# First product of nine of twelve token pairs as seven products of half sums, the verdict on VectorE and TensorE, and zeros in tiles of three PSUM groups

## The chip, the cores and the metric

The kernel runs on one core of a Trainium2 chip. A core has TensorE (PE in the profile; its weight loads are listed apart as PEld), VectorE (DVE), ScalarE (ACT), GpSimd (POOL) and SyncE (SP), which issues most of the DMAs. The metric is the device time of one execution in microseconds, lower is better. The kernel before took 631.13 us, the median of three runs (629.88, 631.13 and 631.83).

## The reference

Attention over a window, then a feed forward product over its output. Everything is fp32; batch 4, 8 heads, 768 positions, head dimension 64, so that `x` has 3072 tokens of 512 values. `n_global` is 8 and `n_local` is 96.

```python
scores = scale * np.matmul(q, k.transpose(0, 1, 3, 2))        # 4 x 8 x 768 x 768
keep = is_global | is_local                                   # first 8 keys, or the last 96
scores = np.where(keep, scores + bias, -1e9)                  # bias = -slope(head) * distance
a = np.exp(scores - max); a = a / (a.sum(-1) + 1e-9)
x = (a @ v) as 3072 x 512
h = x @ w_in                                                  # 512 -> 2048
g = np.where(h >= 1, h, np.where(h <= -1, 0, (h + 1) ** 2 / 4))
out = (g @ w_out).astype(np.float32)                          # 2048 -> 512
```

`w_in` and `w_out` arrive as float64.

## The kernel before, in words

**Tiles.** A unit is 128 query rows of one batch with all 8 heads, and there are 24. The first unit of each batch (units 0 to 3) sees 128 keys and is computed in fp32 (`first_scores`, `first_turn`, `first_av`, `first_xt`). The other 20 see 256 keys and are computed with each fp32 number as two fp16 numbers, a high and a low part, so that one product becomes three matmuls (high by high, high by low, low by high). A unit is worked in two halves of four heads: `scores` (L757, 24 matmuls of 128 columns on 64 rows), `masked` (L578, VectorE), `expo` (L590, ScalarE, which also adds up the row sums with an accumulator), `split_p` (L773 high part on ScalarE, L775 low part on VectorE), `turn_p` (a DMA transpose, L782), `attend` (L800, 24 matmuls of 64 columns), `norm` (L602), `scale_x` (L642), `split_x` (L814, L816) and `turn_x` (DMA transpose).

Two units make a pair of 256 tokens, and there are twelve. For each pair `ffn1` (L885) computes `h` in 8 groups, each with 24 matmuls of 256 columns (2 slices of 128 outputs, 4 of 128 inputs, 3 products of parts) into one PSUM tile of the group `ps_h`. `gelu` takes a tile through ScalarE (L898), VectorE (L903, L908), ScalarE (L912, the high part) and GpSimd (L916, the low part). `ffn2` (L928) multiplies by `w_out`: per pair 2 token blocks of 16 slices of 3 matmuls of 512 columns into `ps_o`. `finish` (L945, L943, L948) scales and stores.

**Weights.** The float64 weights come in 32 pieces (`w_load` L466), are put together from their two halves with integer operations on VectorE (`w_bits` L480, L484, L487), and split (`w_hi` L500 and `w_scale` L507 on ScalarE, `w_lo` L514 on GpSimd). While that goes on, the first pairs of FFN1 and FFN2 follow the pieces. From then on the pieces are loaded a second time for tests of their range (`check_load` L541, `check_reduce` L546).

**Order.** Every step is put into a list with a due time (`at`), and the list is run in the order of a written table of indices, `PLACE` (lines 103 to 249). The order of each engine's instructions is the order in that table. Nothing is reordered at run time; an instruction waits for its inputs and for its tile, and what stands behind it on its engine waits too. `filler` (L443) issues a matmul of zeros of 128x512 into the tile `spare`, which nobody reads, between the first steps.

**Verdict.** The kernel holds for inputs within bounds. At the end (L282 to L308) VectorE compares all recorded maxima with their limits, GpSimd reduces over partitions (L304), and one register is loaded (L308); if it is set, a general path is run, which is not the case here.

The lines the change touches:

Of the kernel before, what the change touches and what calls it, by code (L numbers as in the profile page):

```python
# [39 lines left out]
SC = SQK * SQK  # L40

# [4 lines left out]
NSU = NU // 2 * (NFC // 2)  # L46

NQ = "scalar"
WENG = "a"
INS = 6  # L50
F32B = 7
PSH = 2
PSO = 2
HB = {"k": 3, "q": 2, "v": 3}
HE = {"k": "p", "q": "p", "v": "v"}
KGE = "vector"
XL = "v"
# [263 lines left out]
def fast_path(ctx, tc, q, k, v, nraw, nval, w_in, w_out, out, half, nm, sums, sq, su):  # L321
# [900 lines left out]
```

## Time and profile before

| what | value |
|---|---|
| median of three runs | 631.13 us |
| span of the profiled execution, first to last instruction | 629.1 us |
| PE busy | 615.7 us, 98% |
| DVE busy | 448.0 us, 71% |
| ACT busy | 418.7 us, 67% |
| POOL busy | 239.5 us, 38% |
| granted TensorE clock, mean over the span | 0.999 |

The page gives for the profiled execution no time other than its span; the median of the runs is 2.0 us longer. A row of the page's fifth part names the source line, the engine, the operation and its tiles, then the busy time and the mean duration of one instruction, then the engine's idle time just before these and what ended it. Matmuls overlap, so the mean duration of a matmul (380 ns for 512 columns) is longer than the distance from one start to the next; the timeline shows the distance. In the timeline the first number is the start, the second the duration, and a bracket at the end names the idle time before the row.

### The profile page before, as it was taken

What the parts mean: (1) busy time and instruction counts of PE and PEld (TensorE: products, weight loads), DVE (VectorE), ACT (ScalarE), POOL (GpSimd) and SP (SyncE); (2) the same over time, 40 slices, a digit from 0 to 9 for tenths busy, and PEclk for the clock granted to TensorE, in tenths of its full rate; (3) what the DMA queues carried; (4) which work ended last, traced back from release to release, by engine and by line L of the source; (5) the groups of instructions that cost most, each with busy time, mean ns of one, the idle gap of its engine ahead of it and who ended that gap; (6) DMA issues with size and microseconds to landing.
All of it is one profiled execution on the core that took longest, in us unless ns stands there. A gap on an engine that the chain in (4) does not pass through costs nothing. (4 is left out here: it accounts for less than half of the span.)

```text
span 629.1 us, 14881 instructions
## 1 busy us (share of the span) xinstructions
PE 615.7 (98%) x5665; PEld 420.8 (67%) x5665; DVE 448.0 (71%) x1150; ACT 418.7 (67%) x1070; POOL 239.5 (38%) x226
## 2 busy tenths in 40 slices
PE   7999999899999999999999999999999999999996
PEld 4676666556876767767757667667667767767652
DVE  6889999987676656665777777777777686663440
ACT  4778898997777776676686776766866765632220
POOL 0336786650544424433443333425324421122210
PEclk9999999999999999999999999999999999999999
DMA  6847566597533553464395497586476455361121
GB/s 201 261 144 225 187 227 221 129 170 157 126 87 77 91 121 93 80 148 111 69 231 154 94 208 186 127 186 175 110 177 183 112 140 137 76 150 69 51 69 38
DMA packets 144227, 88.08 MB, mean 140 GB/s; under 512 B 108180, under 2 KB 124820, under 8 KB 144148
## 3 DMA queue, kind: packets, MB, share of 16 engines
q1 hardware_dynamic: 144000, 86.92, 55.4%
q8 instruction: 46, 0.75, 0.5%
q14 instruction: 33, 0.27, 0.1%
q10 hardware_dynamic: 148, 0.13, 0.1%
HBM read 54.53 MB, written 6.29 MB: 97 GB/s over the span
## 5 line engine op out<-in xcount | busy, mean ns | idle before, releaser
L885 PE MATMUL h<-xt,wih 128*128 128x256 f16 x1536 | 256.4, 273 | 1.0 <-DVE u L908 0.9
L916 POOL TENSOR_TENSOR gl<-u,gh 128x512 f16<-128x512 f32 x96 | 117.4, 1224 | 284.9 <-ACT gh L912 274.6
L885 PE MATMUL h<-xt,wil 128*128 128x256 f16 x768 | 209.4, 273 | 0.0
L885 PEld LDWEIGHTS <-wih 128*128 128x128 f16 x1536 | 147.4, 98 | 30.9 <-DVE u L908 1.6
L928 PE MATMUL o<-wol,gh 128*128 128x512 f16 x384 | 145.6, 379 | 1.3 <-POOL wol L514 1.2
L928 PE MATMUL o<-woh,gh 128*128 128x512 f16 x384 | 145.8, 380 | 0.0
L928 PE MATMUL o<-woh,gl 128*128 128x512 f16 x384 | 145.6, 379 | 0.0
L928 PEld LDWEIGHTS <-gh 128*128 128x128 f16 x768 | 71.8, 98 | 67.3
L903 DVE SCALAR_TENSOR_TENSOR h<-h,u 128x512 f32<-128x512 f32 x96 | 66.7, 694 | 68.2 <-ACT u L898 68.0
L590 ACT ACTIVATE z<-z,nm 128x256 f32<-128x256 f32 (+1 forms) x192 | 91.7, 479 | 14.9 <-DVE nm L578 14.3
L912 ACT ACTIVATE gh<-u 128x512 f16<-128x512 f32 x96 | 60.2, 627 | 60.4 <-DVE u L908 60.1
L898 ACT ACTIVATE u<-h,half 128x512 f32<-128x512 f32 x96 | 64.9, 676 | 43.3 <-PE h L885 43.2
L578 DVE CUSTOM_DVE_ANT_0 z<-s,bias 128x256 f32<-128x256 f32 (+1 forms) x192 | 67.2, 396 | 26.6 <-PE s L757 23.2
L885 PEld LDWEIGHTS <-wil 128*128 128x128 f16 x768 | 75.0, 98 | 8.8
L775 DVE SCALAR_TENSOR_TENSOR ph<-z,ph 128x1024 f16<-128x1024 f32 x40 | 60.0, 1499 | 22.1 <-ACT ph L773 21.8
L928 PEld LDWEIGHTS <-gl 128*128 128x128 f16 x384 | 37.5, 98 | 47.2 <-issue 2.2
L908 DVE SCALAR_TENSOR_TENSOR u<-u,h 128x512 f32<-128x512 f32 x96 | 65.3, 681 | 3.3 <-DVE good L298 0.3
L546 DVE TENSOR_REDUCE sq<-c_raw 128x1 f32<-128x256 f32 x128 | 48.6, 408 | 0.2
L773 ACT ACTIVATE ph<-z 128x1024 f16<-128x1024 f32 x40 | 42.0, 1050 | 0.7
L757 PEld LDWEIGHTS <-qh 64*128 64x128 f16 x960 | 26.9, 94 | 16.7 <-issue 9.5
L800 PEld LDWEIGHTS <-pt 128*128 128x128 f16 x960 | 33.4, 98 | 7.0
L590 ACT ACTIVATION_READ_ACCUMULATOR z<-z,nm 128x1 f32 x192 | 36.0, 187 | 0.0
(101 smaller groups left out, 676.6 us busy)
## 6 DMA issues: line engine op xcount, KB each, us to landing
w_raw<-in_moe_w_in_dram SPq DMA_DIRECT2D x16, 512.0 KB, 3.8
w_raw<-in_moe_w_out_dram SPq DMA_DIRECT2D x16, 512.0 KB, 3.7
c_raw<-in_moe_w_in_dram SPq DMA_DIRECT2D x32, 256.0 KB, 3.5
c_raw<-in_moe_w_out_dram SPq DMA_DIRECT2D x32, 256.0 KB, 3.1
vr<-in_v_dram SPq DMA_DIRECT2D x28, 256.0 KB, 3.5
kr<-in_k_dram SPq DMA_DIRECT2D x28, 256.0 KB, 3.7
qr<-in_q_dram SPq DMA_DIRECT2D x24, 256.0 KB, 4.0
out_dram<-ob SPq DMA_DIRECT2D x23, 256.0 KB, 3.0
```

The costliest lines, as they stand in the source:

```text
L546: nc.vector.tensor_reduce(sq[:, col : col + 1], tops[n, e], axis=AX.X, op=op, apply_absolute_value=True)
L578: nc.vector.tensor_tensor_reduce(out=p32[u, hf][:, hh, :], in0=pts[u, hf][hh // 2][:, hh % 2, 0:n], in1=bias[:, 4 * hf + hh, base : base + n],
L590: nc.scalar.activation(z, z, AF.Exp, bias=nm[:, c : c + 1], scale=-1.0, accum_out=sums[:, c : c + 1])
L773: nc.scalar.activation(phs[u, hf][:, 0, :], zf, AF.Copy, scale=SP_)
L775: nc.vector.scalar_tensor_tensor(phs[u, hf][:, 1, :], zf, SP_, phs[u, hf][:, 0, :], op0=ALU.mult, op1=ALU.subtract)
L885: nc.tensor.matmul(hp[:, e, :], w[:, dc, f], xt[:, hf, 2 * a + j, :], start=(n == 0), stop=(n == 3 * NDC - 1),)
L898: nc.scalar.activation(us[c, g], hs[c, g], AF.Relu, bias=half, scale=2.0 / (SV * SW), accum_out=su[:, col : col + 1])
L903: nc.vector.scalar_tensor_tensor(ws[c, g], hs[c, g], 4.0 / (SV * SW), us[c, g], op0=ALU.mult, op1=ALU.max)
L908: nc.vector.scalar_tensor_tensor(dst, us[c, g], 4.0, ws[c, g], op0=ALU.min, op1=ALU.mult)
L912: nc.scalar.activation(gh, ws[c, g], AF.Copy)
L916: (nc.gpsimd if GL == "p" else nc.vector).tensor_sub(gl, ws[c, g], gt[c, g][0])
L928: nc.tensor.matmul(po, a[:, cs], w[:, f, :], start=(f == 0 and n == 0), stop=(f == NFC - 1 and n == 2))
```

## The change

For pairs 3 to 11 `ffn1` is replaced by `product`, `keep` and `join`. The tokens of the pair are cut into two blocks of 128, the 512 inputs into two halves of 256, and the 256 outputs of a pair of slices into two of 128; seven products of sums of these blocks take the place of eight. Each half pair (`j`, 1024 of the 2048 outputs) has seven products of 24 matmuls of 128 columns, listed as p1, p5, p2, p6, p3, p7, p4; the table sets which of them come next to each other and what stands between. Four of the seven (p6, p7 and p4 in the tile of p1, p3 in that of p5) are accumulated on an earlier product in the same PSUM tile; p7's sum with p5 is written by VectorE into a fourth tile, and p4, which is accumulated in the tile that p7 used, follows that. `keep` copies a product to SBUF on ScalarE, `join` adds it on VectorE. Pairs 0 to 2 keep `ffn1`.

The sums have to be made: of the weights once (`t_sum` and `t_mix` on GpSimd, 8 and 32 instructions, `t_hi` on ScalarE, `t_lo` on VectorE, 8 x 2 each), of `x` for each of the nine pairs (`mix_x`, four instructions on GpSimd of 128x256). The parts of `x` are split into `xa` (128x512, the unchanged blocks) and `xb` (128x1280, the sums), with the low parts on GpSimd and no longer on VectorE, and each is turned by a DMA transpose.

Beside that: the row sums of units 4 to 23 come from a 65th column of ones in `attend`, not from an accumulator; the accumulator of `gelu`'s first step is gone; `turn_p` is two transposes, one behind each part; the PSUM group `ps_b` is gone and `ps_h` has 3 tiles; pairs 0 and 1 take FFN2 together while the weights arrive; fillers write tiles of three PSUM groups in turn and wait for these like any other step; and the verdict stands in the table, on VectorE, with a matmul on TensorE for the sum over partitions. The general path is not changed.

```diff
+FIRSTW = 3
+PRODUCTS = ("p1", "p5", "p2", "p6", "p3", "p7", "p4")
+XLO = "gpsimd"
+TMIX = "gpsimd"
+TLO = "vector"
...
-    ps_b = pool("ps_b", 1, space=PSUM)
-    ps_h = pool("ps_h", PSH, space=PSUM)
+    ps_h = pool("ps_h", 3, space=PSUM)
...
+    def filler(tag, n):
+        shape = [P, 2, WIN] if tag == "s" else [P, DM]
+        spare = {"s": ps_s, "h": ps_h, "o": ps_o}[tag].tile(shape, F32, tag=tag, name=f"spare_{tag}{n}")
...
+    def t_mix(g, n):
+        t = tsum[g]
...
+        b11, b12, b21, b22 = t[:, 0:2, 0], t[:, 0:2, 1], t[:, 2:4, 0], t[:, 2:4, 1]
+        dst, x, y = ((b11, b12, b11), (b12, b22, b12), (b22, b22, b11), (b21, b21, b22))[n]
+        getattr(nc, TMIX).tensor_sub(dst, x, y)
...
-        av = ps_av.tile([P, 4, D], F32, tag="av", name=f"av{u}_{hf}")
+        av = ps_av.tile([P, 4, D + 1], F32, tag="av", name=f"av{u}_{hf}")
...
+    def mix_x(c, n):
...
+        a11, a12, a21, a22, s1 = (xs[c][:, e, :] for e in range(5))
+        if n == 0:
+            nc.gpsimd.tensor_add(s1, a21, a22)
+        elif n == 1:
+            nc.gpsimd.tensor_sub(a21, a11, a21)
...
+    def product(c, j, name):
...
+        for m in range(4):
+            g = 4 * j + m
+            n = 0
+            for dc in range(2):
+                for a, b in ((0, 0), (0, 1), (1, 0)):
...
+                    nc.tensor.matmul(
+                        hp[:, m, :], w, xf(b, dc), start=(fresh and m == n == 0),
...
+    def keep(c, j, name):
...
+        s = mid.tile([P, 4 * P], F32, tag="m", name=f"s{name}_{c}_{j}")
+        nc.scalar.activation(s, flat(hs[c, j, {"p1": "a", "p6": "a", "p5": "b"}[name]]), AF.Copy)
...
+    def join(c, j, t):
+        slot, name, prod = {11: ("c", "p1", "p2"), 12: ("b", "p6", "p3"), 22: ("a", "p5", "p7")}[t]
...
+        if t == 22:
+            dst = flat(ps_h.tile([P, 4, P], F32, tag="h", name=f"h{c}_{j}d"))
...
+        nc.vector.tensor_add(dst, h, sc[c, j, name])
...
-    nc.gpsimd.partition_all_reduce(anybad, worst, channels=P, reduce_op=bass_isa.ReduceOp.max)
...
+    def sentence():
+        total = ps_av.tile([1, 1], F32, tag="av", name="total")
+        nc.tensor.matmul(total, worst[:, 0:1], worst[:, 1:2], start=True, stop=True)
+        nc.vector.tensor_single_scalar(badi, total, 0.5, op=ALU.is_ge)
```

The table `PLACE` is new throughout. Three places of the order that it sets, in the instructions as each engine gets them (line, operation, result<-operands, size of the result, and the queues of which a wait is written on the instruction):

On TensorE before, at the end of the second product of pair 6 (`o6_1`) and the beginning of the first product of pair 7 (`h7_6`):

```order
L928 LDWEIGHTS gh6_6_5536
L928 MATMUL o6_1_5621<-wol_119,gh6_6_5536 128x512
L928 LDWEIGHTS gl6_6_5569
L928 MATMUL o6_1_5621<-woh_118,gl6_6_5569 128x512
L885 LDWEIGHTS wih_116 [waits DVE_49]
L885 MATMUL h7_6_6199<-xt7_5071,wih_116 128x256 [waits PE_49]
```

TensorE after, at the place where p4 of pair 7's first half begins; six matmuls of FFN2 stand between it and the last matmul of p7, and the rows show the last two of them (`tt0_1` are half sums of weights, `xtb7` the turned sums of `x`, `h7_0a` the tile that p7 was accumulated in):

```order
L1039 LDWEIGHTS gh6_1_22_6604
L1039 MATMUL o6_1_6482<-wol_117,gh6_1_22_6604 128x512
L1039 LDWEIGHTS gl6_1_22_6605
L1039 MATMUL o6_1_6482<-woh_116,gl6_1_22_6605 128x512
L972 LDWEIGHTS tt0_1_1056
L972 MATMUL h7_0a_6571<-xtb7_6598,tt0_1_1056 128x128 [waits DVE_49]
```

Both times products of FFN1 follow matmuls of FFN2 of pair 6. Before, a new tile begins there, which waits for an earlier `gelu`; after, p4 goes on in the tile of p7 and waits for the join on VectorE that reads it.

On VectorE before, a stretch of the steady part (pair 7, units 16 to 18; `ph` is the low part of the probabilities):

```order
L775 SCALAR_TENSOR_TENSOR ph17_0_5953<-z17_0_5912,ph17_0_5953 128x1024 [waits DMAHW1_49,Activation_49]
L903 SCALAR_TENSOR_TENSOR h7_3_5917<-h7_3_5917,u7_3_5966 128x512 [waits Activation_49]
L642 TENSOR_TENSOR x16_1_6004<-av16_1_5971,r16_1_5740 128x256 [waits PE_49]
L908 SCALAR_TENSOR_TENSOR u7_3_5966<-u7_3_5966,h7_3_5917 128x512 [waits DVE_49,Pool_49]
L742 COPY vh16_3_5248<-vg2_4547 32x1024
L816 TENSOR_TENSOR xh16_1_6010<-x16_1_6004,xh16_1_6010 128x256 [waits DMAHW2_49,Activation_49]
L707 SCALAR_TENSOR_TENSOR vh18_5_6000<-vr18_5_5786,vh18_5_6000 128x512 [waits DMAHW5_49]
```

VectorE after, a like stretch (pair 7, units 18 and 19):

```order
L701 SCALAR_TENSOR_TENSOR vh19_0_7357<-vr19_0_7196,vh19_0_7357 128x8x64 [waits DMAHW7_49,Activation_49]
L997 TENSOR_TENSOR h7_1d_7407<-h7_1a_7027,sp5_7_1_7128 128x512 [waits PE_49]
L731 COPY vg3_7417<-vh19_0_7357 32x1040 [waits DVE_49,Pool_49]
L493 TENSOR_REDUCE sq_69<-c19_0_raw_7267 128x1
L1012 SCALAR_TENSOR_TENSOR h7_1d_7407<-h7_1d_7407,u7_1_22_7420 128x512 [waits Activation_49]
L493 TENSOR_REDUCE sq_69<-c19_1_raw_7294 128x1 [waits DMAHW5_49]
L775 SCALAR_TENSOR_TENSOR ph18_0_1_7481<-z18_0_7322,ph18_0_0_7447 128x1024 [waits DMAHW0_49,Activation_49]
L1014 SCALAR_TENSOR_TENSOR u7_1_22_7420<-u7_1_22_7420,h7_1d_7407 128x512 [waits DVE_49,Pool_49]
```

Joins (L997) stand between the steps of `gelu` and of attention, and the low half of `x` (L816) is gone from this engine.

On VectorE before, the end of the program (`good` and `worst` are the verdict, `ob` the last store):

```order
L298 TENSOR_SCALAR good_9090<-peak_9091 128x16 [waits DVE_49]
L301 TENSOR_REDUCE worst_9103<-good_9090 128x1 [waits DVE_49]
L302 TENSOR_SCALAR worst_9103<-worst_9103 128x1 [waits DVE_49]
L306 CAST badi_9108<-anybad_9106 128x1 [waits Pool_49]
L943 TENSOR_SCALAR ob11_1_9069<-o11_1_9015 128x256 [waits Activation_49]
```

VectorE after, its end (the join and the last steps of `gelu` of pair 11, then the threshold of the sum and the last store):

```order
L1110 MEMSET worst_70 128x1
L1111 TENSOR_REDUCE worst_70<-good_10549 128x1 [waits DVE_49]
L1112 TENSOR_SCALAR worst_70<-worst_70 128x1 [waits DVE_49]
L997 TENSOR_TENSOR h11_1d_10626<-h11_1a_10373,sp5_11_1_10459 128x512 [waits PE_49]
L1012 SCALAR_TENSOR_TENSOR h11_1d_10626<-h11_1d_10626,u11_1_22_10631 128x512 [waits Activation_49]
L1014 SCALAR_TENSOR_TENSOR u11_1_22_10631<-u11_1_22_10631,h11_1d_10626 128x512 [waits DVE_49,Pool_49]
L1012 SCALAR_TENSOR_TENSOR h11_1a_10373<-h11_1a_10373,u11_1_21_10662 128x512 [waits Activation_49]
L1014 SCALAR_TENSOR_TENSOR u11_1_21_10662<-u11_1_21_10662,h11_1a_10373 128x512 [waits DMAHW3_49,DVE_49]
L1117 TENSOR_SCALAR badi_71<-total_10740 1x1 [waits PE_49]
L1054 TENSOR_SCALAR ob11_1_10743<-o11_1_10622 128x256 [waits Activation_49]
```

The verdict's comparisons moved from behind all of pair 11 to a place ahead of its last join, and what waits for another engine at the very end is the threshold (L1117), for a matmul.

## Rows read from the trace of the kernel before

**Rows 1.** The page's first part for two engines, busy time, share of the span and instructions, and the granted clock of TensorE in 40 slices, in tenths.

```profile
PE 615.7 (98%) x5665; PEld 420.8 (67%) x5665; DVE 448.0 (71%) x1150; ACT 418.7 (67%) x1070; POOL 239.5 (38%) x226
...
PEclk9999999999999999999999999999999999999999
```

**Rows 2.** Busy time of the engines by stretch: length, then for each engine busy time and instructions, the granted clock, the DMA share and GB/s.

```profile
core 0: us, PE busy (x) PEld busy (x) DVE busy (x) ACT busy (x) POOL busy (x), PEclk, DMA share, GB/s
0.00:40.00 40.00, 35.91 (x210) 23.86 (x211) 30.92 (x133) 24.62 (x78) 8.38 (x12) 1.00 0.67 211
40.00:80.00 40.00, 38.67 (x284) 27.52 (x283) 39.47 (x85) 33.15 (x79) 26.95 (x26) 1.00 0.62 198
80.00:127.00 47.00, 44.74 (x417) 30.58 (x416) 45.63 (x96) 44.38 (x107) 32.85 (x29) 1.00 0.62 187
127.00:178.00 51.00, 50.90 (x565) 35.67 (x562) 38.62 (x102) 41.57 (x112) 21.05 (x21) 1.00 0.74 149
...
0.00:178.00 178.00, 170.23 (x1467) 117.63 (x1468) 154.65 (x413) 143.72 (x373) 89.23 (x87) 1.00 0.66 184
178.00:624.00 446.00, 445.49 (x4200) 303.17 (x4198) 292.97 (x737) 275.02 (x698) 150.23 (x139) 1.00 0.52 123
```

**Rows 3.** TensorE's timeline where the third pair's FFN1 ends (177.60) and in a stretch of the steady part.

```profile
177.60 0.27 PE L885 MATMUL h<-xt,wil 128*128 128x256 f16 x1
177.71 0.38 PE L928 MATMUL o<-woh,gh 128*128 128x512 f16 x1
...
202.31 0.86 PE L800 MATMUL av<-vh,pt 128*128 128x64 f16 x24
203.01 0.38 PE L928 MATMUL o<-woh,gh 128*128 128x512 f16 x1
...
204.31 0.38 PE L885 MATMUL h<-xt,wih 128*128 128x256 f16 x2
...
206.93 0.38 PE L928 MATMUL o<-woh,gh 128*128 128x512 f16 x1
...
209.30 0.38 PE L928 MATMUL o<-woh,gl 128*128 128x512 f16 x1
209.62 0.84 PE L757 MATMUL s<-kh,qh 64*128 64x128 f16 x24
210.39 0.39 PE L885 MATMUL h<-xt,wih 128*128 128x256 f16 x2
```

**Rows 4.** TensorE's groups by line and shape: instructions, busy time, mean ns of one, idle time before.

```profile
L885 PE MATMUL h<-xt,wih 128*128 128x256 f16 x1536 | 256.4, 273 | 1.0 <-DVE u L908 0.9
L885 PE MATMUL h<-xt,wil 128*128 128x256 f16 x768 | 209.4, 273 | 0.0
L928 PE MATMUL o<-woh,gh 128*128 128x512 f16 x384 | 145.8, 380 | 0.0
L800 PE MATMUL av<-vh,pt 128*128 128x64 f16 x960 | 34.5, 193 | 0.0
L800 PEld LDWEIGHTS <-pt 128*128 128x128 f16 x960 | 33.4, 98 | 7.0
L757 PE MATMUL s<-kh,qh 64*128 64x128 f16 x960 | 33.8, 217 | 0.0
L443 PE MATMUL spare<-zeros 128*128 128x512 f16 x109 | 30.5, 413 | 0.0
```

**Rows 5.** Groups of the other engines by line and shape, in the same columns.

```profile
L903 DVE SCALAR_TENSOR_TENSOR h<-h,u 128x512 f32<-128x512 f32 x96 | 66.7, 694 | 68.2 <-ACT u L898 68.0
L816 DVE TENSOR_TENSOR xh<-x,xh 128x256 f16<-128x256 f32 x40 | 19.4, 486 | 0.6 <-ACT xh L814 0.6
L775 DVE SCALAR_TENSOR_TENSOR ph<-z,ph 128x1024 f16<-128x1024 f32 x40 | 60.0, 1499 | 22.1 <-ACT ph L773 21.8
L912 ACT ACTIVATE gh<-u 128x512 f16<-128x512 f32 x96 | 60.2, 627 | 60.4 <-DVE u L908 60.1
L590 ACT ACTIVATION_READ_ACCUMULATOR z<-z,nm 128x1 f32 x192 | 36.0, 187 | 0.0
L898 ACT ACTIVATION_READ_ACCUMULATOR u<-h,half 128x1 f32 x96 | 18.4, 192 | 0.0
L916 POOL TENSOR_TENSOR gl<-u,gh 128x512 f16<-128x512 f32 x96 | 117.4, 1224 | 284.9 <-ACT gh L912 274.6 <-issue 6.4 <-PE o L928 3.9
```

**Rows 6.** The timeline of all engines from the last matmul of an FFN1 group to the first two steps of its `gelu`.

```profile
410.87 0.27 PE L885 MATMUL h<-xt,wil 128*128 128x256 f16 x1
...
411.18 0.69 ACT L898 ACTIVATE u<-h,half 128x512 f32<-128x512 f32 x1 [0.36 <-PE h L885]
411.76 0.19 ACT L898 ACTIVATION_READ_ACCUMULATOR u<-h,half 128x1 f32 x1
411.99 0.70 DVE L903 SCALAR_TENSOR_TENSOR h<-h,u 128x512 f32<-128x512 f32 x1 [0.52 <-ACT u L898]
```

**Rows 7.** The same timeline a little earlier, where VectorE's low part of the probabilities lies beside work of GpSimd, and that line's shortest, median and longest duration in ns.

```profile
406.39 1.16 POOL L713 TENSOR_TENSOR qh<-qr,qh 128x512 f16<-128x512 f32 x1
406.58 2.05 DVE L775 SCALAR_TENSOR_TENSOR ph<-z,ph 128x1024 f16<-128x1024 f32 x1 [1.08 <-ACT ph L773]
...
L775 DVE SCALAR_TENSOR_TENSOR ph<-z,ph x40: 1215/1226/2124, 108.3 to 550.2; 128x1024 f16<-128x1024 f32 x40
```

**Rows 8.** The timeline of the end, without FFN2, and a group of the program's start (a matmul of one row that VectorE reads).

```profile
613.38 0.38 POOL L304 PARTITION_ALL_REDUCE anybad<-worst  x1 [5.97 <-issue]
613.79 0.15 DVE L306 CAST badi<-anybad 128x1 int32<-128x1 f32 x1 [4.54 <-POOL anybad L304]
...
623.59 0.38 ACT L945 ACTIVATE ob<-o 128x256 f32<-128x256 f32 x1 [9.76 <-PEq L308]
...
L394 PE MATMUL pps_n<-nlow,bias 1*128 1x2 f32 x2 | 0.6, 359 | 1.2 <-DVE nlow L392 1.2
```

More of the change, by code (lines that the diff above doesn't have):

```diff
@@ L399, in distances @@
     def distances(own):
+        after("positions")
+        did.add(("dist", own))
         n = P if own else WIN
@@ L402, in distances @@
         m = zp.tile([P, 3, n], F32, tag="z", name=f"m{n}")
-        dist, gap, cut = (m[:, j] for j in range(3))
+        dist, gap = m[:, 0], m[:, 1]
         here = prow[:, 0:1] if own else prow[:, 1:2]
@@ L413, in clip @@
     def clip(own):
+        after("limits", ("dist", own))
+        did.add(("clip", own))
         n = P if own else WIN
@@ L473, in w_bits @@
         if s == 0:
-            if num < NFC and num % 2 and not TPO:
-                wbits[n] = spare(1).bitcast(I32).rearrange("p (a b) -> p a b", a=NDC)
-            else:
-                wbits[n] = ps_b.tile([P, *hi.shape[1:]], I32, tag="b", name=f"w{num}_bits")
+            p, tag = (ps_o, "o") if num < NFC and num % 2 >= BODD else (ps_h, "h")
+            wbits[n] = p.tile([P, *hi.shape[1:]], I32, tag=tag, name=f"w{num}_bits")
         t = wbits[n]
@@ new lines, in split_b, with turn_b @@
+    def split_b(c, lo):
+        after(*(("mix", c, n) for n in range(4)))
+        did.add(("xb", c, lo))
+        src = xs[c].rearrange("p a b -> p (a b)")
+        xbs[c, lo] = xp.tile([P, 5 * 4 * D], F16, tag=f"xb{lo}", name=f"xb{c}_{lo}")
+        if not lo:
+            nc.scalar.activation(xbs[c, 0], src, AF.Copy)
+        else:
+            low(XLO, xbs[c, 1], src, xbs[c, 0])
+    def turn_b(c, lo):
+        after(("xb", c, lo))
+        did.add(("xtb", c, lo))
+        if c not in xtbs:
+            xtbs[c] = xp.tile([P, 2, 5, 2, P], F16, tag="xt", bufs=2, name=f"xtb{c}")
+        nc.sync.dma_start_transpose(
+            out=xtbs[c][:, lo].rearrange("p b j d -> p (b j) d"), in_=xbs[c, lo]
+        )
@@ L919, in ffn2 @@
[L919 to L931 removed]
+        nm_ = f"{c}_{g}" if isinstance(g, int) else f"{c}_{g[0]}_{g[1]}"
@@ new lines, in ffn2 @@
+    def ffn2(c, t, f, n):
+        if c < FIRSTW:
+            g, e = divmod(f, 2)
+            key, cs = g, slice(e * CH + t * P, e * CH + (t + 1) * P)
+        else:
+            j, m = divmod(f, NFC // 2)
+            m, e = divmod(m, 2)
+            key, cs = (j, 10 * (t + 1) + e + 1), slice(m * P, (m + 1) * P)
+        after(("w", NFC + f), ("g", c, key, 4))
+        if n == 0:
+            p, tag = (ps_h, "h") if c == 1 else (ps_o, "o")
+            os_[c, t] = p.tile([P, DM], F32, tag=tag, name=f"o{c}_{t}")
+        gh, gl = gt[c, key]
+        for i, (a, w) in enumerate(((gh, woh), (gh, wol), (gl, woh))):
+            nc.tensor.matmul(
+                os_[c, t], a[:, cs], w[:, f, :], start=(n == 0 and i == 0), stop=(n == NFC - 1 and i == 2)
+            )
+        if n == NFC - 1:
@@ new lines, in fast_path @@
+    for J in range(J0, 2 * NCH):
+        first = J == J0 and FIRSTW == 2
+        tj[J + 1] = tj[J] + (11.5 if first else PJ)
+    for c in range(FIRSTW + 1, NCH + 1):
+        starts[c] = tj[2 * c]
+    for J in range(J0, 2 * NCH):
+        c, j = divmod(J, 2)
+        t, dt = tj[J], (tj[J + 1] - tj[J]) / 7
+        for n, name in enumerate(PRODUCTS):
+            tp = t + dt * n
+            at(tp, product, c, j, name)
+            if name in ("p1", "p5", "p6"):
+                at(tp + 1.5, keep, c, j, name)
+            d = {"p2": 11, "p3": 12, "p7": 22, "p4": 21}.get(name)
+            if d:
+                if d != 21:
+                    at(tp + 1.6, join, c, j, d)
+                put_gelu(c, (j, d), tp + 2.2)
+        last = J + 1 == 2 * NCH
+        t, dt = tj[J + 1] + 1.5, 0.66 if last else PJ / 16
+        order = [(x, e, m) for x in range(2) for e in ((0, 1) if x == 0 else (1, 0)) for m in range(4)]
+        for n, (x, e, m) in enumerate(order):
+            at(t + dt * n, ffn2, c, x, 8 * j + 2 * m + e, 8 * j + n % 8)
+            if j == 1 and n % 8 == 7:
+                put_finish(c, t + dt * n + 0.8, x)
```

766 lines of the change are left out of this document (420 added, 346 removed), and 308 rows, old and new, of tables (PLACE, k).

## The prediction

> **What bounds the kernel now.** I read the engines' shares first. TensorE is busy 98% of the span with the clock granted in full; VectorE has 71%, ScalarE 67%, GpSimd 38% [rows 1]. An average can hide stages, so the stretches come next [rows 2]. From 178 us to 624 TensorE is busy 445.49 of 446.00 us. Before that it is busy 170.23 of 178.00, fillers included, and VectorE has 85.10 of 87.00 us between 40 and 127, where the weights are converted. So there are two stages: the first, up to the end of the third pair's FFN1 at 177.7 [rows 3], shared by TensorE and VectorE; and the second, TensorE alone.
>
> Since matmuls overlap, their cost is the distance of starts, not the mean duration in the groups [rows 4]. The timeline gives it [rows 3]: 24 matmuls of 256 columns from 204.31 to 206.93, 109.2 ns each; 11 distances of 512 columns in 2.37 us, 215.5 ns each; 24 of `attend` (64 columns, a weight load each) in 0.70 us, 29.2 ns; 24 of `scores` in 0.77 us, 32.1 ns, or 64.2 for the two that share the row groups. With these, the second stage before is 960 x 0.2155 + 1728 x 0.1092 + 744 x 0.0321 + 768 x 0.0292 = 206.9 + 188.7 + 23.9 + 22.4 = 441.9 us (the counts add up to the 4200 of [rows 2]). It took 445.9 (177.7 to 623.6), so 4.0 are lost to everything else.
>
> **FFN1 of the nine pairs.** It removes 9 x 192 matmuls of 256 columns (188.7 us) and adds 9 x 14 x 24 = 3024 of 128, a shape in fp16 over 128 rows that the trace lacks. A line through 256 and 512 columns is 2.9 ns + 0.415 ns per column; at 64 columns it says 29.5, and the row of `attend` is 29.2. So 56.0 ns at 128, and 169.3 us: 19.4 less. Bounds: from below, no fixed part, 0.415 x 128 = 53.1 ns (8.7 us less again); from above, the pair of `scores`, 64.2 ns, 24.8 us more. The change breaks even on this term at 188.7 / 3024 = 62.4 ns. I take 56.0, since the row of `attend` has the same weight load for half the columns at half the price: a load of 98 ns [rows 4] does not hold up matmuls that come every 29.2 ns.
>
> The Trainium skill, "TensorE: Matmul & The Clock Gate", section "Back-to-back issue gap", says otherwise: in a stream of loads and matmuls 128 columns would sustain about 81 ns and 512 about 131. By that, an estimate from the page, the products would take 244.9 us and the kernel about 685. The trace disagrees at 512 (215.5 ns) and has 64 columns well under it; no run yet shows 128.
>
> **`attend`.** 65 columns by the line are 29.9 ns against 29.2; I take 29.6: 792 matmuls, 23.4 us. Bounds 0 and +0.6 us.
>
> **The second stage after.** 966 FFN2, 3024 products, 744 scores, 792 of `attend`: 208.2 + 169.3 + 23.9 + 23.4 = 424.8 us. To the loss of 4.0 come 2 for the new waits, see below: 430.8 against 445.9.
>
> **The wait of p4.** p4 goes on in the tile of p7 only when the join has read it. Between them stand six matmuls of FFN2, 1.29 us. The chain is the drain of p7's last matmul, the start of VectorE (0.31 us from the last matmul's start to ScalarE's first step in [rows 6]), the join (one pass of 128x512 out of PSUM, 0.69 us as L903 in [rows 5]) and the way back to TensorE, for which I take the 0.04 us by which VectorE follows ScalarE's read [rows 6]. That is about 1.05 us, so some 0.2 to spare where VectorE is free. Queued behind p4 on TensorE is all else, scores and FFN2 too. Ahead of the join on VectorE can stand a low part of the probabilities, 1.23 us, or 2.05 beside GpSimd [rows 7]; then p4 waits up to 1.85. These passes fill 60.0 us [rows 5], 13% of the stage's 446, so by chance 2 or 3 of the 18 joins meet one, with 0.8 us of it left on the mean: 2 us, which I take. The lower end is 0; the upper, all 18 behind the longest pass, is 33 us, far from the 4.0 that the stage before loses to all its waits.
>
> **Other engines in the second stage.** VectorE gains 54 joins (37.3 us) and 16 `t_lo` (11.0) and loses 40 low parts of `x` (19.4): 448 to about 477 us, 79% of the new span. ScalarE gains 54 `keep` and 16 `t_hi` (70 x 0.63 = 43.9) and loses 96 accumulator reads of `gelu` (18.4) and 160 of 192 of the exponentials (30): about the same. GpSimd gains 40 half sums of weights, 36 of `x` and the low parts; from 1224 ns for 512 columns [rows 5] and 8 instructions of 1024, 68 of 256, 11 of 512 and 9 of 1280 columns that is 102 us, with some small fills 105: 345, 57%. None becomes the bound in sum; TensorE covers all of it. If that cover goes, it is by lateness of single steps, which is a rival below. The sums of `x` and their transposes are placed most of a pair's time (430.8 / 9 = 47.9 us) ahead of their use.
>
> **The first stage.** Counted from the order, it holds the same 576 FFN1 matmuls of 256 columns and 216 scores, 186 FFN2 instead of 192, 168 `attend` instead of 192, and 86 fillers where before there are 109. At the prices above (fillers 215.5) before is 140.3 of 177.7 us, 37.4 for the fp32 units and waits; after is 133.4. With the same 37.4 the stage ends at 170.8, 6.9 earlier. VectorE has much the same work there, 154.65 us and about 1.5 more, and 9.1 idle in the first 40 us [rows 2]: 165. So TensorE still ends last, but by little. Bounds: fillers only fill waits, so their saving may be nothing, and VectorE's 1.5 may come on top: 179.2; or both engines pack as VectorE allows: 165.
>
> **The verdict and the end.** Before, the reduction of GpSimd starts at 613.38 and its result is there by 613.94, while TensorE runs to the last store's start at 623.59 [rows 8]: taking it away gains nothing. After, some 15 short instructions (3 us at the 0.15 of L306, with the longer reduction) stand on VectorE ahead of the last join, beside FFN2 on TensorE. At the very end come a one-row matmul (0.36 us as L394) and a threshold (0.15 as L306): +0.5, bounds 0 and 1. The last 5.5 us, store included, stay.
>
> **Sum.** 170.8 + 430.8 + 5.5 + 0.5 = 607.6 us of span against 629.1: 21.5 less. The median stands 2.0 above the span, so 609.6.
>
> **Rivals.** *Waits in the chain of joins.* For it: seven products go through three tiles and a fourth, the slack is 0.2 us, GpSimd's work, half as much again, makes VectorE's longest pass more often 2.05. Against: most of VectorE's idle time remains. At 0.8 us in each of 18 half pairs 14.4 us more: 624. It decides itself on the count of late joins.
>
> *The start is VectorE's.* For it: 85.10 of 87.00 us there. The stage gains nothing and costs 1.5 more: 609.6 + 8.4 = 618.
>
> *A short matmul costs what `scores` cost* (slower side). At 64.2 ns in all 3024 products of the second stage the gain of 19.4 becomes a loss of 5.4: 609.6 + 24.8 = 634.4. From 63.1 ns on (56.0 + 21.5 / 3.024) nothing of the whole gain is left. For it: each product matmul has a load of its own, and FFN1 before had one per 256 columns. Against: the row of `attend`, and that the 64.2 are two matmuls. The section of the Trainium skill named above goes further the same way.
>
> *Better.* Waits at 0, 53 to 55 ns: about 600.
>
> That the change does not do what it says would need fewer columns not to be fewer: 3024 x 128 is 387,000 against 442,000, so it does.
>
> **How the numbers follow.** Forecast (609.6, itself 600 to 616) 0.70; waits 0.12; start 0.07; slower 0.08; better 0.03. A measurement tells 0.3% from nothing, 629.2 to 633.0. Of the waits' 0.12, 0.03 lie there (0.8 us becoming 1.1 or more), of the slower case 0.01. So faster 0.89, same 0.04, slower 0.07. The range 600 to 626 holds the forecast, the start, and most of the waits; it leaves out the slower case, the far waits and half of better, some 0.13.
>
> **What would show it.** Distances of product matmuls at 56 ns in the timeline, and 169 us for the nine pairs: the first term. The third pair's FFN1 over by about 171: the second. Idle time before L972 that VectorE's join ended, about 2 to 4 us in all: the third; over 10 means the waits. The verdict's rows done before TensorE's last FFN2 matmul. Wrong would be a distance above 60 ns, a first stage that ends at 178, or idle time of TensorE in the second stage of over 10 us.

## The result and the profile after

The changed kernel took 619.98 us, the median of four runs (617.98 to 623.54), beside 630.5 for the kernel before: a ratio of 0.984, interval 0.981 to 0.988. Two later series of the same kernel gave 618.45 (0.982, 0.979 to 0.984) and 619.91 (0.984, 0.981 to 0.987). It is faster, by 10 to 13 us (1.6 to 1.8%), where 21.5 were forecast.

The page of the profiled execution (623.54 us, the longest of its four) begins as [rows 1] do; the clock is again by slices:

```profile
span 621.6 us, 17389 instructions
...
PE 593.3 (95%) x6942; PEld 421.7 (68%) x6942; DVE 479.2 (77%) x1188; ACT 425.7 (68%) x864; POOL 361.5 (58%) x369
...
PEclk9999899999999999999999999999999999999997
```

TensorE's busy time fell by 22.4 us, the span by 7.5: the work went, and idle time came. VectorE has 479 us where 477 were forecast, GpSimd 361.5 where 345 were. The windows show the place; they answer to [rows 2], with the same columns, and the last is the stage behind the third pair's FFN1:

```profile
0.00:40.00 40.00, 30.40 (x195) 21.47 (x196) 30.49 (x126) 23.82 (x72) 8.41 (x12) 1.00 0.66 205
40.00:80.00 40.00, 35.28 (x282) 27.39 (x282) 37.72 (x82) 30.51 (x75) 28.03 (x26) 0.96 0.44 142
80.00:127.00 47.00, 46.35 (x398) 30.22 (x394) 45.59 (x90) 36.33 (x73) 40.59 (x42) 1.00 0.70 179
127.00:178.00 51.00, 48.51 (x527) 33.05 (x523) 45.88 (x105) 43.44 (x90) 44.93 (x44) 1.00 0.70 161
181.00:612.00 431.00, 428.93 (x5522) 306.73 (x5519) 317.32 (x782) 288.20 (x552) 236.58 (x246) 1.00 0.62 140
```

TensorE is busy 160.5 of the first 178 us (before 170.2), and 428.9 of 431.0 behind them. The borders of the stages come from the timeline, here that of `again` (615.7 us of span, the changed kernel profiled a second time): the last matmuls of the third pair's FFN1, and the start of the last store's scaling.

```profile
177.40 0.27 PE L935 MATMUL h<-xt,wil 128*128 128x256 f16 x1
177.51 0.28 PE L800 MATMUL av<-vh,pt 128*128 128x65 f16 x4
...
607.47 0.39 ACT L1056 ACTIVATE ob<-o 128x256 f32<-128x256 f32 x1 [4.58 <-PE o L1039]
```

| part of the sum | before | forecast | after | again |
|---|---|---|---|---|
| first stage, to the third pair's FFN1 | 177.7 | 170.8 | 180.7 | 177.5 |
| second stage, to the last store's scaling | 445.9 | 430.8 | 432.1 | 430.0 |
| from there to the end | 5.5 | 6.0 | 8.8 | 8.2 |
| span | 629.1 | 607.6 | 621.6 | 615.7 |

The large term came as forecast. What failed is the first stage, which gave back nothing, and the end, which cost 3 us.

A stretch of the second stage in the changed kernel's timeline has the shape that the kernel before lacked:

```profile
400.26 0.27 PE L972 MATMUL h_1a<-xta,wih 128*128 128x128 f16 x2
400.37 0.22 PE L972 MATMUL h_1a<-xta,wil 128*128 128x128 f16 x1
...
401.60 1.50 PE L972 MATMUL h_1b<-xtb,tt 128*128 128x128 f16 x24
402.94 1.22 PE L972 MATMUL h_1a<-xtb,tt 128*128 128x128 f16 x19
```

24 matmuls from 400.26 to 401.60, and 24 to 402.94: 55.8 ns each (the last row's 19 are those that start before the window's end at 404). All waits of TensorE in this stage are one line of the view of waits from 181 to 612 us (in total, times, the longest; in `again` it is 0.6 us, once):

```profile
PE av L800 <- DMA pt<-ph: 2.0, 4, 0.7
```

### The profile page after: what moved, and what is told of

It is laid out like the page before. It is cut to its first block, busy times and chain, and to the rows that moved or that the text cites. A ratio compares the mean times of both kernels' runs of the same rounds, so it can differ in the third digit from the quotient of the medians.

```text
span 621.6 us, 17389 instructions
## 1 busy us (share of the span) xinstructions
PE 593.3 (95%) x6942; PEld 421.7 (68%) x6942; DVE 479.2 (77%) x1188; ACT 425.7 (68%) x864; POOL 361.5 (58%) x369
## 4 chain that ended last, share of the span: by engine, by line
PE 70%; POOL 8%; DVE 7%; DMA 5%; ACT 5%; issue 3%; SPq 0%; POOLq 0%; DVEq 0%; ACTq 0%
PE o L1039 30%; PE h_0a L972 7%; PE h_1a L972 7%; PE h L935 5%; PE h_0b L972 4%; PE av L800 4%; PE h_1b L972 3%; PE s L756 3%; DMA pt<-ph 3%; PE h_0c L972 2%; PE h_1c L972 2%; POOL tsum L512 1%; PE av L613 1%; POOL g L1023 1%; POOL wol L462 1%
## 5 line engine op out<-in xcount | busy, mean ns | idle before, releaser
L1039 PE MATMUL o<-woh,gh 128*128 128x512 f16 x352 | 133.6, 380 | 0.0
L1039 PE MATMUL o<-woh,gl 128*128 128x512 f16 x352 | 133.4, 379 | 0.0
L1039 PE MATMUL o<-wol,gh 128*128 128x512 f16 x352 | 133.4, 379 | 0.0
L972 PEld LDWEIGHTS <-tt 128*128 128x128 f16 x1728 | 100.4, 98 | 10.4 <-issue 0.2
L559 DVE CUSTOM_DVE_ANT_0 z<-s,bias 128x256 f32<-128x256 f32 x160 | 64.9, 414 | 16.4 <-PE s L756 16.4
L972 PEld LDWEIGHTS <-wih 128*128 128x128 f16 x864 | 66.9, 98 | 4.5 <-DVE u L1014 0.3
L935 PE MATMUL h<-xt,wih 128*128 128x256 f16 x384 | 65.5, 277 | 4.1 <-DVE w_f L438 3.4
L935 PE MATMUL h<-xt,wil 128*128 128x256 f16 x192 | 53.2, 277 | 0.0
L935 PEld LDWEIGHTS <-wih 128*128 128x128 f16 x384 | 38.0, 100 | 10.4 <-issue 4.0
L972 PEld LDWEIGHTS <-wil 128*128 128x128 f16 x432 | 42.3, 98 | 0.0
L462 POOL TENSOR_TENSOR wil<-w_f,wih 128x512 f16<-128x512 f32 x16 | 18.8, 1174 | 39.5 <-ACT w_f L457 39.5
L972 PE MATMUL h_0a<-xtb,tt 128*128 128x128 f16 x648 | 40.6, 219 | 0.0
L972 PE MATMUL h_1a<-xtb,tt 128*128 128x128 f16 x648 | 40.6, 219 | 0.0
```

The lines of the kernel that those rows point to most:

```text
L462: nc.gpsimd.tensor_sub(lo, wf[n], hi)
L559: nc.vector.tensor_tensor_reduce(out=p32[u, hf][:, hh, :], in0=pts[u, hf][hh // 2][:, hh % 2, 0:n], in1=obias[hf][:, hh, :] if own else bi ...
L935: nc.tensor.matmul(hp[:, e, :], w[:, dc, f], xt[:, a, dc, :], start=(n == 0), stop=(n == 3 * NDC - 1))
L972: nc.tensor.matmul(hp[:, m, :], w, xf(b, dc), start=(fresh and m == n == 0), stop=(m == 3 and n == 5), skip_group_check=not fresh,)
L1039: nc.tensor.matmul(os_[c, t], a[:, cs], w[:, f, :], start=(n == 0 and i == 0), stop=(n == NFC - 1 and i == 2))
```

## The experiments

Each of the next is told with what it changes in the changed kernel; several are built on `early_sentence`, and say so.

### The changed kernel again, and the end

`again` and `again_five` are the changed kernel without an edit. The first was expected as follows:

> The changed kernel as it is, for a second profile and an interval on the chip of the next three. Both theories: the same time as before in the two-sided sense of 618 to 622 us, the third pair's FFN1 over at 177 to 181 us, and 8 to 9 us from the last matmul to the end.

It took 618.45 us; the stages are in the table. The second stood beside `early_five`:

> The changed kernel once more, five rounds, to stand beside the next on one chip: 617.5 to 620 us.

It took 619.91 us.

`early_sentence` moves one entry of the order, ahead of 13 steps of FFN2 of three matmuls each:

```diff
+    last = [n for n in order if plan[n][2] is sentence][0]
+    order.remove(last)
+    tail = [i for i, n in enumerate(order) if plan[n][2] is ffn2]
+    order.insert(tail[-13], last)
```

> Only the verdict's matmul and threshold move: ahead of the last 39 matmuls of FFN2, not behind them. Theory of the branch (TensorE's own load of the verdict and its branch, 4.3 us, lie behind the last matmul now and lay beside FFN2 before): the time from the last matmul to the end falls from 8.8 to about 5.5 us, 3 us less in all. Rival (the end is the last store's landing, 3.9 us after its issue): 0.5 us less at most, the matmul and the threshold alone.

616.64 us (ratio 0.978, 0.974 to 0.981) against 618.45 (0.979 to 0.984). As these intervals overlap, both were run again, five rounds side by side:

> early_sentence once more, five rounds. Theory of the branch: 2.5 to 3.3 us less than the run beside it (8.5 us from the last matmul to the end become 5.7). Rival (what the end gains the stages before it lose, as the first look at it, 1.8 us less with intervals that overlap, allows): less than 1 us.

615.99 us (0.977, 0.975 to 0.980) against 619.91 (0.981 to 0.987): 3.9 us less, and intervals apart. So the late verdict does cost the end some 3 to 4 us, a little more than the theory's 2.5 to 3.3, and the rival's "less than 1" fell. The theory gives TensorE's branch as the reason. The view of the branch's line shows it; its rows name the engine's queue, the instruction, its duration in ns (shortest, median, longest) and its first and last start. First before, then after, then `early_five`:

```profile
L308 PEldq COMPARE_BRANCH  x1: 3342/3342/3342, 620.1 to 620.1; - x1
```

```profile
L260 PEldq COMPARE_BRANCH  x1: 4290/4290/4290, 613.6 to 613.6; - x1
```

```profile
L260 PEldq COMPARE_BRANCH  x1: 3607/3607/3607, 606.3 to 606.3; - x1
```

All engines branch on the verdict. TensorE's branch is listed with 3.3 to 4.3 us, the others' with 0.05 to 0.07. Before, TensorE's queue came to it at 620.1, while matmuls that were already handed over ran to 623.3; it was over as these were. After, the verdict is known only at 612.97 (the threshold behind the last matmul), so the branch begins at 613.6 with nothing to run beside it. In `early_five` the threshold stands at 601.15, the branch runs from 606.3 to 609.9, and the last matmul starts at 609.25:

```profile
600.92 0.19 PE L1116 MATMUL total<-worst 128*1 128x1 f32 x2
601.15 0.14 DVE L1117 TENSOR_SCALAR badi<-total 1x1 int32<-1x1 f32 x1 [3.80 <-PE total L1116]
...
609.25 0.38 PE L1039 MATMUL o<-woh,gl 128*128 128x512 f16 x1
```

This version beats both kernels.

Two rows of the end do not fit a branch of TensorE alone. VectorE's next instruction, too, stands 3.6 us behind its short branch (3.3 before and in `early_five`):

```profile
L260 DVEq COMPARE_BRANCH  x1: 72/72/72, 613.8 to 613.8; - x1
L260 DVEq EVENT_SEMAPHORE  x1: 21/21/21, 617.4 to 617.4; - x1
```

And TensorE is late once more behind its branch. These are the last instructions of VectorE and of TensorE in the changed kernel, then of TensorE before and in `early_five`:

```profile
L1413 DVEq EVENT_SEMAPHORE  x2: 21/21/21, 619.3 to 619.8; - x2
L1413 PEldq EVENT_SEMAPHORE  x2: 51/51/51, 619.3 to 621.6; - x2
```

```profile
L1220 PEldq EVENT_SEMAPHORE  x2: 51/51/51, 628.6 to 629.1; - x2
```

```profile
L1418 PEldq EVENT_SEMAPHORE  x2: 51/51/51, 614.7 to 615.3; - x2
```

In the changed kernel TensorE's last start is 1.7 us behind VectorE's (1.2 in `again`); before and in `early_five` it is at most 0.1 behind. So of the 2.7 to 3.3 us that the end became longer, 1.2 to 1.7 are this second delay. Between 619 and 622 us the only DMA packet is one of 16 KB on the queue of instructions (q8), and such a packet lies beside the branch as well. That both delays are loads of instructions is therefore likely, but no run tests it.

### The first stage: one engine at a time

Four theories were tried for the first stage: that it is TensorE's own (fillers and all), that the half sums on GpSimd delay the weights, that VectorE's sum of work sets it, and that ScalarE's does.

`no_fillers`:

```diff
+    order = [n for n in PLACE if plan[n][2] is not filler]
```

> Leaves out the 86 matmuls of zeros between the first steps, whose tiles nobody uses. Rival (the first stage is TensorE's own, and fillers that wait for their tiles block it): 86 x 0.2155 = 18.5 us of work go, 5 to 18 us less. Theory of the preparation: fillers only fill waits, so the time stays within 2 us, idle time on TensorE in the first 130 us grows by about 15 us, and the granted clock there may fall.

625.26 us, 5 to 7 slower than the changed kernel, outside both expectations. Less work on TensorE made it longer: its granted clock reads 0.93 between 127 and 178 us, where the changed kernel has 1.00 (between 40 and 80 both have 0.96), and the third pair's FFN1 ends at 184.4. So the fillers fill waits, and without them the clock fell once more; 0.07 of 51 us are 3.6, and what the rest is stays open.

`light_tensor` takes useful work away instead:

```diff
-                for w, a in ((wih, 0), (wih, 1), (wil, 0)):
+                for w, a in ((wih, 0), (wih, 1), (wil, 0))[: 2 if c < 2 else 3]:
```

> Leaves out the third product (low part of the weights) in FFN1 of pairs 0 and 1, 128 matmuls of 256 columns or 14.0 us on TensorE beside the weights' conversion. Theory of VectorE: within 2 us of the changed kernel's 618.5, with TensorE idle for longer ahead of the last weight. Rival (TensorE sets the first stage's end): 10 to 14 us less.

617.91 us. The last matmul of the third pair's FFN1 starts at 177.26; in `again` it was 177.40. 14.0 us of TensorE's work ahead of the last weight are worth nothing. Part of them came back as slower matmuls, since the clock fell where `again` has 1.00:

```profile
40.00:80.00 40.00, 32.40 (x236) 23.37 (x237) 38.38 (x91) 32.32 (x79) 29.96 (x28) 0.91 0.48 152
```

0.09 of 40 us are 3.6; the other ten brought nothing either. The forecast's term is of this kind: its 6.9 us were 23 fillers (5.0), 6 matmuls of FFN2 (1.3) and 24 of `attend` (0.7).

`no_sums`:

```diff
-        getattr(nc, TSUM).tensor_add(t.rearrange("p a b c -> p a (b c)"), wih[:, :, fs], wil[:, :, fs])
+        nc.gpsimd.memset(t, 0.0)
...
-        getattr(nc, TMIX).tensor_sub(dst, x, y)
```

> Leaves out the half sums of the weights: of 40 additions on GpSimd there remain 8 fills with zeros; all products run on zeros. Theory of the preparation (the first stage ends when GpSimd and VectorE have prepared the weights, and the half sums stand among them): third pair's FFN1 over at 171 to 174 us instead of 180.7, the last low part of a weight at 125 to 135 instead of 151; 6 to 9 us less in all. Rival (the first stage is TensorE's own): within 1.5 us of the changed kernel.

619.2 us, and the last low part of a weight still at 149.1. The half sums do stand among the weights on GpSimd and on the chain of waits, and taking them away brings nothing.

`light_vector` adds to it:

```diff
-        low(TLO, tt[g, e][:, 1], tsum[g][:, 2 * e : 2 * e + 2], tt[g, e][:, 0])
+        nc.gpsimd.memset(tt[g, e][:, 1], 0.0)
...
+        elif u < 8:
+            nc.gpsimd.memset(ph, 0.0)
```

> Leaves out what no_sums does, and takes two kinds of work that are no part of the weights' own conversion off VectorE: the low parts of the half sums (16 of 0.7 us) and the low parts of the probabilities of units 4 to 7 (8 of 1.2 to 2 us) become fills of zeros on GpSimd. Theory of VectorE (it is busy 97% up to the last weight and paces the first stage by its sum of work): some 20 us go from it there, so the last weight's low part comes at 128 to 138 us instead of 149, the third pair's FFN1 is over at 164 to 172 instead of 178.5, 6 to 14 us less in all than no_sums. Rival (the weights' own chain of load, three passes, ScalarE and GpSimd sets their pace): within 2 us of no_sums.

617.18 us, FFN1's last matmul at 175.08, last low part at 146.1: the edge of the rival's 2 us. But more than half of what it took off VectorE stood behind the last weight (9.6 us were ahead of it), so a larger dose followed.

`two_passes`, on top of `early_sentence`:

```diff
-            nc.vector.scalar_tensor_tensor(t, rh, -0x40000000, t, op0=ALU.bitwise_and, op1=ALU.bitwise_or)
+            pass
...
-            nc.vector.scalar_tensor_tensor(f, rl, 29, t, op0=ALU.logical_shift_right, op1=ALU.bitwise_or)
+            nc.vector.scalar_tensor_tensor(f, rh, -0x40000000, t, op0=ALU.bitwise_and, op1=ALU.bitwise_or)
```

> early_sentence, and of VectorE's three passes over each weight piece the middle one takes the last one's place, so that the lowest three bits of each fp32 weight are left out: 32 passes of 0.68 us, 22 us, all ahead of the last weight. Theory of VectorE (it is busy 95% from 20 us to the last weight; light_vector took only 9.6 us off it ahead of that weight, the rest came behind it): last pass over a weight at 120 to 128 us instead of 141.6, third pair's FFN1 over at 162 to 169 instead of 177.8, 8 to 15 us less than early_sentence's 616.6. Rival (TensorE, ScalarE and GpSimd are near enough to full, and the order couples them, so half of it or more comes back as waits): last pass at 130 to 136, FFN1 over at 171 to 175, 3 to 6 us less.

614.13 us, 2.5 less than `early_sentence`; last pass at 138.0, FFN1's last matmul at 174.23. 22 us less on VectorE, all ahead of the last weight, and 3.6 of them arrive at FFN1's end, less than even the rival expected (the intervals of the two times overlap). With TensorE's 14 us away as well:

> two_passes, and the third product (low part of the weights) of FFN1 of pairs 0 and 1 left out, 14.0 us on TensorE ahead of the last weight. If TensorE is what bounds once VectorE is relieved: 3 us or more less than two_passes. Rival (it is the order's waits, or VectorE still): within 2 us of two_passes.

612.8 us, FFN1 over at 175.8: within 2 us, as the rival said, but with the granted clock at 0.94 between 20 and 80 us and 0.91 between 80 and 120, where `two_passes` has 1.00.

`light_scalar`, on top of `early_sentence`, leaves out ScalarE's second pass over the weights:

```diff
-        nc.scalar.activation(wf[n], wf[n], AF.Copy, scale=SW)
```

> early_sentence without ScalarE's second pass over each weight piece (the scaling ahead of the low part, 32 of 0.62 us, 20 us; the low parts of the weights are then wrong in size). Theory of ScalarE (82% busy in every run so far and lightened in none, it paces the weights): last weight's low part at 125 to 138 us instead of 149, 5 to 12 us less than early_sentence's 616. Rival (the order written, no engine's sum): 0 to 4 us less, last low part at 143 to 147.

619.13 us, about 3 more than without the edit, which neither theory expected: by itself it is worth nothing either. The granted clock is 0.94 between 20 and 80 us, where `early_sentence` has 1.00; 0.06 of 60 us are 3.6.

The other direction was tried with an exchange: one VectorE pass (0.69 us) of 16 weight pieces for one on ScalarE and one on GpSimd, on top of `early_sentence`:

```diff
-        return WS[n % len(WS)] == "s"
+        return n < NFC
...
+            w_sign(n) if signed(n) else None
```

> early_sentence, and the 16 pieces of the first weight matrix lose one of three passes on VectorE (0.69 us each, 11 us) for a pass on ScalarE and one on GpSimd (0.6 and 1.2 us). Theory of VectorE: 4 to 11 us less than early_sentence's 616.6. Rival (all three engines are as full as each other there): within 2 us, or more.

636.5 us, 20 more. `sign_odd` does the same for every second piece:

> The same exchange for every second piece of both weight matrices. Theory of VectorE: 4 to 11 us less than early_sentence's 616.6; as GpSimd is busy 47 of 51 us between 127 and 178, less of it than in sign_first. Rival: within 2 us, or more.

631.59 us, 15 more. The theory of VectorE missed both times, and the rival had said "within 2 us, or more" without a size. What the groups of `sign_first` by line show is the chain of one piece, now longer by GpSimd's step, for which ScalarE waits:

```profile
L446 POOL TENSOR_TENSOR w_f<-w_f,w_raw 128x512 f32<-128x512 f32 x16 | 20.7, 1291 | 29.9 <-DVE w_f L438 19.5 <-ACT w_f L458 3.8 <-ACT z L570 3.0
...
L452 ACT ACTIVATE wih<-w_f 128x512 f16<-128x512 f32 x16 | 10.1, 629 | 18.4 <-POOL w_f L446 18.4
```

16 steps of 1.29 us are 20.7, and the kernel is 20 us longer; the same 16 steps in `sign_odd`, half of them in each matrix, cost 15. The low part of the first matrix's last piece starts at 97.3 (79.6 in `early_sentence`). VectorE's relief of 11 us does not show. That the length of the step alone makes the 15 to 20 us is argued: the granted clock of `sign_first` is 0.91 between 20 and 80 us.

### The first stage: several at once

`light_both` joins `light_vector` and `light_tensor`:

> Leaves out what light_vector and light_tensor do, both at once: the half sums of the weights, the low parts of the half sums and of the probabilities of units 4 to 7 on VectorE, and 128 matmuls of pairs 0 and 1. Theory of the two (TensorE and VectorE are both full up to the last weight and wait for each other by the order, so that lightening one alone shows the other): the third pair's FFN1 is over at 160 to 170 us, the last weight's low part at 125 to 140; 6 to 14 us less than light_vector's 617.2. Rival (something else paces the weights, ScalarE, GpSimd, the loads or the latency of their chain): within 2.5 us of light_vector, last weight again at 144 to 148.

613.8 us, the median of three executions (a fourth took 3370.35 us; why is not known), FFN1's last matmul at 173.48, last low part at 144.3: 3.4 less than `light_vector`, where the rival had 2.5 at most and the theory 6 or more. `three_light` joins `two_passes` and `light_vector`, `all_light` adds `light_tensor`, `four_light` adds `light_scalar`:

> two_passes and light_vector together: the half sums of the weights left out on GpSimd, and on VectorE one of three passes over the weights, the low parts of the half sums and of the probabilities of units 4 to 7 left out. Theory of the coupled engines (VectorE and GpSimd take turns on the path to the last weight, so that relief of one alone is answered by the other): last pass over a weight at 118 to 130 us, third pair's FFN1 over at 162 to 169 instead of 174.2 (two_passes) and 175.1 (light_vector), 5 to 12 us less than two_passes' 614.1. Rival (neither: TensorE or the latency of the steps in the order written for other loads): last pass at 131 to 137, FFN1 over at 170 to 174, less than 4 us from two_passes.

613.59 us, FFN1's last matmul at 174.71: nearest to the rival's, and later than even its 170 to 174.

> three_light, and the third product of FFN1 of pairs 0 and 1 left out, 14.0 us on TensorE. If TensorE is the bound that is left: 4 us or more less than three_light, third pair's FFN1 over 4 us or more earlier. Rival (the order's own waits): within 2.5 us of three_light, with TensorE idle for longer between 20 and 120 us.

611.0 us, 173.4: 2.6 less, again at the edge. The windows of `all_light` from 20 to 120 us, beside those of `again`, show three engines with time to spare and a stage only 4.0 us shorter (173.4 against 177.4):

```profile
20.00:80.00 60.00, 49.84 (x386) 36.34 (x384) 50.03 (x141) 50.21 (x133) 33.46 (x32) 0.97 0.49 158
80.00:120.00 40.00, 36.46 (x287) 21.72 (x287) 28.81 (x61) 32.08 (x64) 33.31 (x38) 0.96 0.77 191
```

```profile
20.00:80.00 60.00, 54.23 (x446) 41.84 (x445) 57.45 (x147) 47.93 (x124) 37.47 (x35) 1.00 0.50 157
80.00:120.00 40.00, 39.39 (x334) 25.75 (x333) 39.18 (x74) 32.40 (x64) 35.00 (x35) 1.00 0.69 181
```

VectorE idles 21 us of 100, TensorE 14, and what they wait for is each other and ScalarE; the granted clock fell here too (0.97 and 0.96). `all_light`'s longest waits between 20 and 145 us, in total, times and the longest:

```profile
POOL wil L462 <- ACT w_f L457: 26.3, 10, 8.5
DVE h L1014 <- ACT u L1012: 9.9, 10, 2.7
...
PE h L937 <- DVE w_f L438: 7.5, 5, 4.7
ACT woh L451 <- DVE w_f L438: 6.3, 4, 3.2
...
DVE z L559 <- PE s L756: 5.5, 4, 2.6
```

> all_light and light_scalar together: what was left out on GpSimd, VectorE, TensorE and ScalarE, all at once. Theory of ScalarE: 5 us or more less than all_light's 611.0, third pair's FFN1 over at 160 to 168 us instead of 173.4. Rival (the order written): 0 to 4 us less, FFN1 over at 169 to 173.

605.01 us, FFN1's last matmul at 166.75 and the last low part at 137.8: 6.0 less than `all_light`, the numbers of ScalarE's theory, from an edit that by itself brought nothing. So no engine's sum alone sets the first stage. Counted ahead of the last weight, 31 us off VectorE, 12 to 17 off GpSimd, 14 off TensorE and 20 off ScalarE are worth at most 2.5 us one by one and 10 to 12 together (605.0 against 616.6 of `early_sentence`, 0.961 and 0.978 of the kernel before; FFN1's last matmul at 166.75 against 177.8). Each engine runs its instructions in the order written, and each waits in turn for another. That it is this order, and not the share of the clock that was lost in the relieved runs, which keeps the rest is argued from the waits above; no run has another order at the same clock.

`fewer_fillers` is the cheap edit that this picture offered: `early_sentence` without the last 18 fillers, which stand where TensorE is nearly full.

> early_sentence without the last 18 fillers, which stand from about 70 us on, where TensorE is nearly full. Theory of the two: as TensorE is one of two full engines there, 0 to 4 us less than early_sentence's 616.6, and no lower clock. Rival (the fillers only fill waits everywhere, and keep the clock): the same within 1 us, or up to 3 us more with a lower granted clock.

617.4 us (614.63 to 618.95) against 616.64: the same, and FFN1's last matmul at the same place (177.3).

## Why the prediction was half right

**The products.** 55.8 ns in the rows above, 56.0 forecast; the distances from start to start of all 3024 add up to 170.4 us against 169.3. The line through 256 and 512 columns held, and the rival of short matmuls at 64.2 ns fell. The estimate of 81 ns from the Trainium skill ("TensorE: Matmul & The Clock Gate", "Back-to-back issue gap") is not borne out by these rows, though each product matmul has a load of its own.

**The wait of p4.** Forecast 2 us, measured none: TensorE's only waits of note in the second stage are 2.0 us of `attend` (0.6 in `again`) for a transpose of the probabilities. That the sum of the stage (432.1 and 430.0 against 430.8) is right with these and 1.1 us of the products in the place of the joins is luck in that size. The rival of waits in the chain of joins fell.

**The first stage** is the step that failed. "With the same 37.4 the stage ends at 170.8": the 37.4 us were no constant. At the same prices the rest is now 180.7 - 133.4 = 47.3 us, in `again` 44.1. The forecast counted fewer fillers as time saved, though [rows 2] show a VectorE busy 85.10 of 87.00 us beside them; `light_tensor` shows that even 14 us of real work there are worth nothing, and `no_fillers` that fillers' time is needed. It also took VectorE's work in the stage as 1.5 us more, where it is 5.0 to 5.5 (159.68 and, in `again`, 160.16 us in the first 178), and left out GpSimd, which has 33 to 36 us more there (121.96 and 124.98 against 89.23). The rival "the start is VectorE's" foretold the size (618), with the stage gaining nothing. In part that is luck, as it had 1.5 us more for the stage and 0.5 for the end, where 0 to 3 and about 3 came. Its reason does not hold as it stood: VectorE alone relieved of 22 us gave 2.5. What the trace after shows is that the last weight is finished later. The last pass on VectorE and the last low part on GpSimd, first before:

```profile
117.90 0.69 DVE L487 SCALAR_TENSOR_TENSOR w_f<-w_raw,w_bits 128x512 int32<-128x512 int32 x1
120.66 1.16 POOL L514 TENSOR_TENSOR wol<-w_f,woh 128x512 f16<-128x512 f32 x1 [2.76 <-ACT w_f L507]
```

```profile
144.31 0.69 DVE L438 SCALAR_TENSOR_TENSOR w_f<-w_raw,w_bits 128x512 int32<-128x512 int32 x1
151.25 1.56 POOL L462 TENSOR_TENSOR wol<-w_f,woh 128x512 f16<-128x512 f32 x1
```

The new order puts attention and `gelu`, and on GpSimd half sums, ahead of the last weights. The windows up to VectorE's last pass, before and in `again`, in the columns of [rows 2]:

```profile
0.00:117.90 117.90, 110.33 (x779) 75.76 (x780) 107.09 (x287) 93.08 (x239) 65.87 (x64) 1.00 0.65 206
```

```profile
0.00:140.70 140.70, 125.80 (x1018) 86.11 (x1019) 128.91 (x333) 106.62 (x251) 89.65 (x92) 1.00 0.66 187
```

The pass comes 22.8 us later; VectorE has 21.8 us more ahead of it, GpSimd 23.8, TensorE 15.5 and ScalarE 13.5. Behind the last weight TensorE has 28 to 30 us of work left, where before it had 57; so a later weight and a shorter rest cancel, and the stage ends about where it did. A different order might keep the 6.9 us; none was tried, so whether they are to be had stays open.

**The end.** "+0.5, bounds 0 and 1" for the verdict: it cost 2.7 to 3.3 us. The matmul and the threshold were not sized too low (0.36 and 0.15 us forecast, 0.19 and 0.15 in the trace). What the step left out is what follows them: the load of the verdict on each engine, the branches, and TensorE's last instructions, which had been hidden, and which a verdict behind the last matmul exposes. `early_five` shows it for the whole; how it divides among them is not shown. The forecast looked at what was removed (rightly worth nothing) and not at who waits for the result.

**The chances.** Faster had 0.89, and the time lies in the range, towards its upper end, where the range reached for the two rivals of delay.

## What to carry to other kernels

Price a stage by its sums only where one engine is busy through it and the others are not; where three or four are near 80% or above and the order is fixed, as here, a saving on one brought at most 2.5 us, and 16 steps added to the chain of a weight, 20.7 us in sum, cost 15 to 20. Look at the granted clock of a relieved run before its time is read: it fell in most of them. Matmuls that stand in wait-filling places are no cost to be saved. When a result moves to the end, follow every engine that reads it: a branch, and what stands behind it, that was hidden behind handed-over work becomes the tail.

## What the runs showed of the hardware that was not expected

TensorE's branch over the general path is listed with 3.3 to 4.3 us in every profile looked up, the others' with 0.05 to 0.07; but VectorE's next instruction, too, stands 3.3 to 3.6 us behind its branch. In the kernel before, where matmuls that were handed over earlier ran to 623.3, TensorE's cost nothing.

The granted clock of the changed kernel between 40 and 80 us was 1.00 in `again` and 0.96 in `after` and `again_five`, with TensorE busy 35.3 of 40 us in all three; the third pair's FFN1 ended at 177.5 in `again`, at 179.6 in `again_five` and at 180.7 in `after`. In `after` the clock is at its lower level (0.50, 1.2 GHz) from 72.5 to 75.7 us; TensorE had been busy 7.14 of the 10 us up to 72.4, and in `again`, where it did not fall, 7.38. What decides it is open. It is not the whole of the difference between these profiles: the first matmul of FFN1 starts at 32.9 in `again` and at 35.2 in `after`, well ahead of the fall. The row of `after` stands above; these are `again_five` and `again`.

```profile
40.00:80.00 40.00, 35.30 (x290) 27.12 (x290) 37.68 (x83) 30.51 (x74) 28.00 (x26) 0.96 0.45 141
```

```profile
40.00:80.00 40.00, 35.26 (x300) 27.44 (x298) 38.82 (x89) 30.74 (x74) 29.09 (x28) 1.00 0.46 146
```
